# Attention-done pairs take turns with the others in the last loop, with their digits on two halves of the partitions

## The chip, the core and the metric

The kernel runs on one core of a Trainium2 chip. The metric is the device time of one execution in microseconds (us), given as the median of several runs. A profiled execution has a span, which is some 1.8 us shorter than the time of the same run; spans and starts below are from profiles, medians from timed runs.

TensorE multiplies matrices (PE in the profile), VectorE (DVE) and ScalarE (ACT) work on elements, GpSimd (POOL) issues the loads of this kernel, SyncE (SP) the stores. PSUM is the memory that TensorE writes to.

## The reference

```python
# q, k, v: (8 batches, 8 heads, 576, 64); s: (8, 8, 576)
scores = q @ k^T / 8 + min(-(cum_i - cum_j), 0), causal      # cum = cumsum(max(s, 0))
x = softmax(scores) @ v                                      # as (8, 576, 512)
X = rfft(x, axis=1)[:, :64]                                  # 64 modes
Y = X @ (w_r + i w_i), one 512x512 matrix for each mode      # 128 MB of weights
u = x + irfft(Y)
out = u + max(u @ w_ch, 0)                                   # (8, 576, 512)
```

The kernel uses that u @ w_ch = x @ w_ch + irfft(Y @ w_ch). The product x @ w_ch can therefore be made before the last weight of the modes is there, and be kept until Y is complete.

## The kernel before

The output is cut into 18 pairs of row tiles (128 rows each; two of the 18 are tail pairs, made of 64-row ends). Pairs 0 and 1 are done by themselves. The other 16 have their product x @ w_ch kept in SBUF and added back in a last loop. A kept product has one of two forms: fp32, which ScalarE copies back into PSUM ("s"), or two fp16 digits, high and rest, which TensorE adds back with an identity matrix ("e").

```python
ways = dict(zip(kept, "esesessesesseses"))            # kept = pairs 2 to 17

def keep_product(i, xx, z):                            # z is the product in PSUM
    if ways[i] != "e":
        nc.scalar.copy(out=z1s[i][:, xx], in_=z)
        return
    nc.scalar.copy(out=z1s[i][:, 0, xx], in_=z)        # high digit
    nc.vector.tensor_tensor(out=z1s[i][:, 1, xx], in0=z, in1=z1s[i][:, 0, xx], op=ALU.subtract)
```

Attention runs in 32 steps (0 to 31). In the last six, the channel product of a pair that attention has finished is squeezed in, one half before and one half behind the product with the mode weights:

```python
for n in range(N):                                     # N = 32 steps
    load(loads_qkv(n + LA) + tails_due, loads_w(on_chip[n]))   # GpSimd issues
    ...
    av(n, 0)
    if i is not None:
        first_product(i, 0)                            # 4 matmuls, keep_product
        first_transposed(i, 1)
    for c in mode_steps.get(n, []):
        modes(c // NCK, c % NCK)                       # 16 matmuls on 4 weight tiles
    if i is not None:
        first_product(i, 1)
```

All these write into one pool of two PSUM buffers, so the mode product needs the buffer that keep_product is still reading. The weights come in tiles of 512 KB through a ring (WA = 11 tiles at this stage); a tile can be issued only when the mode product has used the one that lay in its place.

The last loop, in which each pair gets its z (the product, relu'd later) and u (x and the inverse transform):

```python
def seed(i):
    ...
    if ways.get(i) == "s":
        nc.scalar.copy(out=zs[i], in_=z1s[i])
    elif ways.get(i) == "e":
        for x in range(2):
            for y in range(2):
                nc.tensor.matmul(zs[i][:, x, :], ident16h, z1s[i][:, y, x, :],
                                 start=(y == 0), stop=False, ...)

for i in range(NPRE, len(pairs)):
    pre(i)                          # seed if "e", then two matmuls of the inverse transform
    start_u(i)
    add_y(us[i], i, 0)
    if ways.get(i + 1) == "s":
        seed(i + 1)                 # on ScalarE, ahead of this pair's relu
    if ways[i] != "v":
        relu(i, 2 if i == last else 1)      # ScalarE
    finish(i)                       # VectorE adds u and the relu, then the store
```

The softmax here doesn't subtract the row's maximum and nothing guards it: scores larger than these inputs give would overflow.

## Time and profile before

| before | value | from |
|---|---|---|
| time, median | 459.26 us (458.73 to 459.38) | 3 runs |
| span of the profiled run | 457.1 us | page |
| last weight lands | 418.07 | load's issue and landing |
| last loop on TensorE | 424.07 to 451.88 | chain of waits |
| mean clock granted to TensorE, 300 to 350 us | 1.00 | stretches |

The table of stretches of the kernel before, over the last steps of attention (stretch in us; then length, busy us and instructions of TensorE, weight loads, VectorE, ScalarE, GpSimd; granted clock; share of the DMA engines; GB/s):

```profile
300.00:320.00 20.00, 17.95 (x258) 12.30 (x258) 13.05 (x27) 11.65 (x22) 10.56 (x15) 1.00 1.31 202
320.00:340.00 20.00, 16.27 (x213) 11.09 (x215) 12.43 (x30) 11.21 (x22) 6.79 (x10) 1.00 1.24 206
340.00:360.00 20.00, 15.76 (x137) 8.56 (x141) 10.94 (x18) 4.04 (x6) 5.94 (x8) 0.91 1.24 212
```

TensorE is busy for 80 to 90% of the time, and the transfers go at 202 to 212 GB/s. TensorE's timeline of the kernel before, the mode products of steps 29 and 30 (start, length, what; in brackets the idle time before it and what ended that):

```profile
316.21 1.12 PE L441 MATMUL yp<-w_sb,xs 128*32 128x512 bf16 x16 [0.45 <-ACT z L491]
...
326.13 1.13 PE L441 MATMUL yp<-w_sb,xs 128*32 128x512 bf16 x16 [0.45 <-ACT z L491]
```

An "s" product lets the mode product go after 0.45 us; behind an "e" product, in steps 28 and 31, the wait was 1.18. GpSimd's timeline of the kernel before, the loads that waited for steps 30 and 31:

```profile
326.92 0.75 POOL L217 DMA_DIRECT2D w_sb<-in_moe_w_i_dram  x1 [5.33 <-PE yp L441]
...
336.58 0.74 POOL L217 DMA_DIRECT2D w_sb<-in_moe_w_i_dram  x1 [5.58 <-PE yp L441]
```

GpSimd waits 5 us for the ring. The tile issued at 326.92 lands at 342.44, 15.5 us later, since five other tiles have still to land ahead of it.

### The profile page before, as it was taken

Reading aid. Unit: us, or ns where it says so; the run is one execution under the profiler, and the core shown is the slowest. Engines: PE = TensorE matmul, PEld = TensorE weight load, DVE = VectorE, ACT = ScalarE, POOL = GpSimd, SP = SyncE. Lnnn points to the kernel's source line nnn. Section 1 sums busy time; section 2 is a strip of 40 time slices with the busy share of each in tenths; the row PEclk is TensorE's granted clock in tenths of the full one; section 3 lists DMA queues with packets and bytes.
Section 4 is the critical chain, followed back from the end, with each engine's and each line's share of the span. In section 5 each row is a group of like instructions: output and inputs, shape, how many; then the busy total and the mean of one; then the engine's idle time right before and its main releaser. Section 6 shows DMA issues by size and latency. Waiting matters only on the chain.

```text
span 457.1 us, 10262 instructions
## 1 busy us (share of the span) xinstructions
PE 339.1 (74%) x4177; PEld 217.2 (48%) x4209; DVE 237.3 (52%) x528; ACT 219.1 (48%) x382; POOL 182.9 (40%) x269
## 2 busy tenths in 40 slices
PE   1779968966562979936587766779967769797995
PEld 1556646644341656614355544446643326343432
DVE  7777645653242556624345544466656425442675
ACT  1587856554241747723445345446622220221895
POOL 6755555544345555344454444355423223200000
PEclk9999999998586889957778799899999778999999
DMA  9999999999999999999999999999999999995688
GB/s 177 201 203 203 202 201 204 202 204 204 204 204 201 202 202 202 204 205 204 199 192 205 204 204 204 204 203 202 207 206 212 210 210 210 214 214 105 235 285 319
DMA packets 109375, 94.54 MB, mean 207 GB/s; under 512 B 28480, under 2 KB 104512, under 8 KB 109328
## 3 DMA queue, kind: packets, MB, share of 16 engines
q0 software_dynamic: 98960, 81.81, 113.0%
q1 hardware_dynamic: 10368, 12.07, 8.5%
q8 instruction: 33, 0.54, 0.4%
q14 instruction: 14, 0.11, 0.1%
HBM read 164.56 MB, written 9.44 MB: 381 GB/s over the span
## 4 chain that ended last, share of the span: by engine, by line
DMA 70%; PE 20%; issue 4%; POOL 3%; DVE 2%; DVEq 0%; POOLq 0%
DMA w_sb<-in_moe_w_i_dram 44%; DMA q<-in_q_dram 13%; DMA w_sb<-in_moe_w_r_dram 5%; PE yp L441 3%; PE sc_ps L365 3%; PE av_ps L394 2%; DMA x_all<-in_moe_w_r_dram 2%; DMA k<-in_k_dram 2%; PE sc_ps L359 2%; DMA y_acc<-in_moe_w_i_dram 2%; PE tr_ps L324 2%; DMA y_acc<-in_moe_w_r_dram 2%; PE u_ps L694 2%; PE z_ps L675 2%; PE u_ps L675 2%
## 5 line engine op out<-in xcount | busy, mean ns | idle before, releaser
L373 ACT ACTIVATE p_sb<-sc_ps,cumt_sb 128x576 f16<-128x576 f32 (+1 forms) x256 | 141.9, 636 | 45.8 <-PE sc_ps L365 45.4
L217 POOL DMA_DIRECT2D w_sb<-in_moe_w_i_dram x60 | 45.1, 751 | 81.7 <-PE yp L441 36.8
L217 POOL DMA_DIRECT2D w_sb<-in_moe_w_r_dram x60 | 45.4, 757 | 65.2 <-DMA w_sb<-in_moe_w_r_dram 26.1
L217 POOL DMA_DIRECT2D v<-in_v_dram x72 | 50.8, 707 | 31.3 <-DMA w_sb<-in_moe_w_r_dram 8.4
L324 PE MATMUL tr_ps<-ident,q 64*64 64x64 bf16 x576 | 17.1, 208 | 55.4 <-DMA q<-in_q_dram 55.4
L359 PE MATMUL sc_ps<-negm,ident 128*128 128x256 bf16 x256 | 55.0, 300 | 0.3
L441 PE MATMUL yp<-w_sb,xs 128*32 128x512 bf16 x480 | 37.0, 408 | 22.2 <-DMA w_sb<-in_moe_w_i_dram 18.1
L327 DVE COPY qtA<-tr_ps 64x576 bf16<-64x576 bf16 x32 | 23.8, 743 | 50.8 <-PE tr_ps L324 50.7
L344 ACT ACTIVATE p<-sc_ps,cumt 128x64 f16<-128x64 f32 x32 | 10.1, 314 | 74.2 <-PE sc_ps L340 74.2
L394 PE MATMUL av_ps<-v,p_sb 128*128 128x65 f16 x1024 | 43.7, 196 | 0.0
L394 PEld LDWEIGHTS <-p_sb 128*128 128x128 f16 x1024 | 38.9, 99 | 4.8 <-issue 0.7
L327 DVE COPY ktA<-tr_ps 64x576 bf16<-64x576 bf16 x32 | 24.0, 750 | 32.7 <-PE tr_ps L324 32.7
L324 PEld LDWEIGHTS <-q 64*64 64x64 bf16 x576 | 13.3, 120 | 58.0 <-DMA q<-in_q_dram 56.9
L441 PEld LDWEIGHTS <-xs 128*32 128x32 bf16 x512 | 22.9, 169 | 32.3 <-issue 28.8
L365 PE MATMUL sc_ps<-qtB,ktB 128*128 128x64 bf16 (+2 forms) x160 | 34.8, 322 | 3.7 <-issue 2.4
L365 PE MATMUL sc_ps<-qtA,ktA 65*128 65x512 bf16 (+2 forms) x192 | 36.1, 297 | 0.3 <-DVE ktA L327 0.3
L399 DVE TENSOR_REDUCE den<-av_ps 128x5 f32<-128x10 f32 x64 | 10.8, 169 | 46.4 <-PE av_ps L394 46.4
L404 DVE TENSOR_TENSOR x_all<-av_ps,rcp 128x320 f16<-128x320 f32 x64 | 31.5, 492 | 2.2
L327 ACT COPY ktB<-tr_ps 64x576 bf16<-64x576 bf16 x32 | 20.3, 634 | 19.7 <-DVE ktA L327 18.8
L365 PEld LDWEIGHTS <-ktB 128*128 128x128 bf16 x192 | 22.4, 117 | 14.8 <-issue 6.3
L324 PE MATMUL tr_ps<-ident,k 64*64 64x64 bf16 x576 | 17.5, 210 | 14.0 <-DVE qtB L327 10.5
L601 PE MATMUL z_ps<-wch_sb,xs 128*128 128x512 f16 x96 | 26.2, 423 | 0.8 <-DVE xs L595 0.8
(112 smaller groups left out, 526.4 us busy)
## 6 DMA issues: line engine op xcount, KB each, us to landing
w_sb<-in_moe_w_r_dram POOLq DMA_DIRECT2D x60, 512.0 KB, 11.9
w_sb<-in_moe_w_i_dram POOLq DMA_DIRECT2D x60, 512.0 KB, 11.9
q<-in_q_dram POOLq DMA_DIRECT2D x32, 144.0 KB, 9.7
k<-in_k_dram POOLq DMA_DIRECT2D x32, 144.0 KB, 10.1
v<-in_v_dram POOLq DMA_DIRECT2D x72, 64.0 KB, 9.7
out_dram<-r_sb SPq DMA_DIRECT2D x16, 256.0 KB, 2.3
out_dram<-r_w SPq DMA_DIRECT2D x16, 256.0 KB, 2.6
x_all<-in_moe_w_i_dram POOLq DMA_DIRECT2D x3, 512.0 KB, 10.0
```

Source lines behind the costliest of these rows:

```text
L217: nc.gpsimd.dma_start(out=dst, in_=src)
L324: nc.tensor.transpose(ps[rows, r, :], src[rows, r, :], ident16[rows, rows])
L327: copy(out=dst[n % NQ][rows, :].rearrange("d (p r) -> d p r", r=R), in_=ps[rows].rearrange("d r p -> d p r"),)
L359: nc.tensor.matmul(ps[:, bass.ds(w * S, W)], ident16, negm[:, bass.ts(r, W)], start=True, stop=False, skip_group_check=True,)
L365: nc.tensor.matmul(ps[:, c0 : c0 + i1 - i0], keys[:, w, r, :], qt[:, i0:i1], start=False, stop=True, skip_group_check=True,)
L373: nc.scalar.activation(out=pt[:, poff[x] : poff[x] + S - w * W], in_=ps[:, w * S : (w + 1) * S - w * W], func=ACTF.Exp, bias=cumt_sb[:, x, ...
L394: nc.tensor.matmul(ps[:, I, r : r + NCH], lhsT, rhs, start=(i == 0), stop=(i == len(todo) - 1), skip_group_check=True,)
L399: nc.vector.tensor_reduce(out=den, in_=ps[:, :, 0 : VW : NCH], axis=mybir.AxisListType.X, op=ALU.add)
L404: nc.vector.tensor_tensor(out=x_all[:, g, b, :, D * h : D * h + D], in0=ps[:, :, 1 : NCH], in1=rcp.unsqueeze(2).to_broadcast([P, NT, D]), ...
L441: nc.tensor.matmul(ps[32 * cg : 32 * cg + 32, :], cols[:, c0 : c0 + 32, c * MC + 2 * cg + par], wt[(g, c, ri, par)][:, cg, :], start=(x == ...
L601: nc.tensor.matmul(z[:, x, :], xts[i][:, x, dt, :], wch_sb[:, dt, :], start=(dt == 0), stop=(last and dt == DT - 1), skip_group_check=True,)
L675: nc.tensor.matmul(dst[x][r, :], G_sb[rows, bass.ds(T * P, r.stop - r.start)], yv[rows, bb, which, :], start=start, stop=True, skip_group_ ...
```

## The change

Its intent is a shorter last loop. An "e" seed costs TensorE four full matmuls. The change introduces a third form, "f": the high digit of rows 0 to 63 lies on the lower half of the partitions and the rest digit of the same rows on the upper half; for rows 64 to 127 it is the other way round. A folding matrix of 128 x 64 adds high and rest in one matmul, and two such matmuls run side by side on two groups of 64 columns. The six pairs whose product is made in attention become "f", one late pair (place 15) is "e", all others are "s"; and the order of the loop is changed so that "f" and "s" pairs alternate.

```diff
+    ident16h_np = np.concatenate([ident_np, ident_np[:, : P // 2] + ident_np[:, P // 2 :]], axis=1)
...
-    pairs = [((b, T), (b, T + 1)) for b in range(B) for T in range(0, NF, 2)]
-    for i, b in ((4, 0), (10, B // 2)):
-        pairs.insert(i, ((b, NF), (b + 2, NF)))
+    turns = [whole[1] + whole[2] + whole[3], whole[4] + whole[5] + whole[6] + whole[7]]
+    turns[1].insert(1, tail_pairs[0])
+    turns[1].insert(5, tail_pairs[1])
+    pairs = list(whole[0])
+    for t in turns[1]:
+        pairs.append(t)
+        if turns[0]:
+            pairs.append(turns[0].pop(0))
...
-    ways = dict(zip(kept, "esesessesesseses"))
+    first_pairs = [i for i in kept if pairs[i][0][0] in (1, 2, 3) and pairs[i][0][1] < NF]
+    ways = {i: "f" if i in first_pairs else "s" for i in kept}
+    for i in (15,):
+        ways[i] = "e"
...
     def keep_product(i, xx, z):
...
+            for y in range(2):
+                own, other = (slice((P // 2) * h, (P // 2) * (h + 1)) for h in (y, 1 - y))
+                nc.scalar.copy(out=z1s[i][own, y, xx], in_=z[own])
+                nc.vector.tensor_tensor(
+                    out=z1s[i][other, y, xx], in0=z[own], in1=z1s[i][own, y, xx], op=ALU.subtract
+                )
...
+        elif ways.get(i) == "f":
+            for x in range(2):
+                for y in range(2):
+                    nc.tensor.matmul(
+                        zs[i][(P // 2) * y : (P // 2) * (y + 1), x, :], fold16h, z1s[i][:, y, x, :],
+                        start=True, stop=False, skip_group_check=True,
+                        tile_position=(0, (P // 2) * y),
+                    )
```

More of the change, by code (lines that the diff above doesn't have):

```diff
@@ L77 @@
     G_np = G_np.reshape(P, SP).astype(np.float16)
-    d_ident16h = nc.inline_tensor(ident_np.astype(np.float16), name="c_ident16h").ap()
+    ident16h_np = np.concatenate([ident_np, ident_np[:, : P // 2] + ident_np[:, P // 2 :]], axis=1)
+    d_ident16h = nc.inline_tensor(ident16h_np.astype(np.float16), name="c_ident16h").ap()
     d_ident32 = nc.inline_tensor(ident_np, name="c_ident32").ap()
@@ L98 @@
     xs = [gp.tile([P, 5, 2, B, NM], BF16, name=f"xs{i}") for i in range(2)]
-    ident16h = gp.tile([P, P], FP16, name="ident16h")
+    ident16h2 = gp.tile([P, P + P // 2], FP16, name="ident16h")
+    ident16h, fold16h = ident16h2[:, :P], ident16h2[:, P:]
     Ff_sb = gp.tile([P, NT, 3 * NM], FP16, name="Ff_sb")
@@ L249 @@
     nc.sync.dma_start(out=Ff_sb, in_=d_Ff.rearrange("(T p) c -> p T c", p=P))
-    nc.sync.dma_start(out=ident16h, in_=d_ident16h)
+    nc.sync.dma_start(out=ident16h2, in_=d_ident16h)
     nc.sync.dma_start(out=G_sb, in_=d_G)
@@ L465, in spread @@
         nc.sync.dma_start(out=yv[16 * c : 16 * c + 16, :, which, :], in_=rows)
-    pairs = [((b, T), (b, T + 1)) for b in range(B) for T in range(0, NF, 2)]
-    for i, b in ((4, 0), (10, B // 2)):
-        pairs.insert(i, ((b, NF), (b + 2, NF)))
+    whole = [[((b, T), (b, T + 1)) for T in range(0, NF, 2)] for b in range(B)]
+    tail_pairs = [((b, NF), (b + 2, NF)) for b in (0, B // 2)]
+    turns = [whole[1] + whole[2] + whole[3], whole[4] + whole[5] + whole[6] + whole[7]]
+    turns[1].insert(1, tail_pairs[0])
@@ L473 @@
+    turns[1].insert(5, tail_pairs[1])
[4 more added lines that the diff above has]
+            pairs.append(turns[0].pop(0))
     NPRE = 2
     kept = list(range(NPRE, len(pairs)))
-    ways = dict(zip(kept, "esesessesesseses"))
-    first_pairs = [i for i in kept[1:] if pairs[i][0][1] < NF and pairs[i][0][0] <= 4][:6]
+    first_pairs = [i for i in kept if pairs[i][0][0] in (1, 2, 3) and pairs[i][0][1] < NF]
+    ways = {i: "f" if i in first_pairs else "s" for i in kept}
@@ L480, with keep_product @@
+    for i in (15,):
+        ways[i] = "e"
     z1s, xts1 = {}, {}
     def kept_place(i, t):
-        if ways[i] == "e":
+        if ways[i] == "s":
+            z1s[i] = t.bitcast(FP32).rearrange("p (x e) -> p x e", x=2)
+        else:
             z1s[i] = t.bitcast(FP16).rearrange("p (y x e) -> p y x e", y=2, x=2)
-        else:
-            z1s[i] = t.bitcast(FP32).rearrange("p (x e) -> p x e", x=2)
-    def keep_product(i, xx, z):
-        if ways[i] != "e":
-            nc.scalar.copy(out=z1s[i][:, xx], in_=z)
-            return
-        nc.scalar.copy(out=z1s[i][:, 0, xx], in_=z)
-        nc.vector.tensor_tensor(out=z1s[i][:, 1, xx], in0=z, in1=z1s[i][:, 0, xx], op=ALU.subtract)
+    def keep_product(i, xx, z):
+        if ways[i] == "s":
+            nc.scalar.copy(out=z1s[i][:, xx], in_=z)
+        elif ways[i] == "e":
+            nc.scalar.copy(out=z1s[i][:, 0, xx], in_=z)
+            nc.vector.tensor_tensor(
+                out=z1s[i][:, 1, xx], in0=z, in1=z1s[i][:, 0, xx], op=ALU.subtract
+            )
+        else:
+            for y in range(2):
+                own, other = (slice((P // 2) * h, (P // 2) * (h + 1)) for h in (y, 1 - y))
+                nc.scalar.copy(out=z1s[i][own, y, xx], in_=z[own])
+                nc.vector.tensor_tensor(
+                    out=z1s[i][other, y, xx], in0=z[own], in1=z1s[i][own, y, xx], op=ALU.subtract
+                )
@@ L800, in seed @@
     def seed(i):
-        if ways.get(i) in ("e", "s"):
+        if ways.get(i) in ("e", "f", "s"):
             zs[i] = zpool.tile([P, 2, DM], FP32, name="z_ps", tag="z")
@@ L811, in seed @@
                     )
+        elif ways.get(i) == "f":
[5 more added lines that the diff above has]
+                        tile_position=(0, (P // 2) * y),
+                    )
     def pre(i):
-        if ways[i] == "e":
+        if ways[i] in ("e", "f"):
             seed(i)
```

## The prediction

> **What bounds the kernel now.** I read the slices of the page first, then the chain that ended last, then the two stretches of that chain which the change touches: the last loop and the last six steps of attention.
>
> ```profile
> DMA  9999999999999999999999999999999999995688
> GB/s 177 201 203 203 202 201 204 202 204 204 204 204 201 202 202 202 204 205 204 199 192 205 204 204 204 204 203 202 207 206 212 210 210 210 214 214 105 235 285 319
> ```
>
> The transfers are busy and move a near constant 200 to 214 GB/s for 36 of 40 slices. The chain, cut to the end, says where that stops:
>
> ```profile
> 396.06 22.01 DMA w_sb<-in_moe_w_i_dram
> 418.07 0.04 issue
> 418.11 0.48 PE yp L441 x4
> ...
> 424.07 0.86 PE z_ps L808 x4
> 424.93 0.43 PE z_ps L675 x2
> 425.36 0.43 PE u_ps L694 x2
> 425.80 0.43 PE u_ps L675 x2
> ...
> 438.51 0.55 PE z_ps L675 x4
> 439.06 0.55 PE u_ps L694 x4
> 439.61 0.55 PE u_ps L675 x4
> 440.16 0.97 PE z_ps L808 x4
> ```
>
> Columns: start, length, what. The last weight lands at 418.07. About 6 us of fixed tail follow, then the last loop (16 kept pairs) from 424.07 to 451.88. The stretches table shows TensorE solid there:
>
> ```profile
> core 0: us, PE busy (x) PEld busy (x) DVE busy (x) ACT busy (x) POOL busy (x), PEclk, DMA share, GB/s
> ...
> 424.07:451.90 27.83, 27.82 (x136) 11.42 (x134) 19.93 (x32) 24.50 (x26) 0.00 (x0) 1.00 0.84 298
> ```
>
> So two regimes: weight arrival until 418, TensorE from 424 to 452, at full clock; 5.2 us of last addition, writing out and ending follow. Work before 418 costs nothing unless it lets the weight queue run empty.
>
> **What the Trainium skill says.** TensorEngine Tiling (Array Packing), Key Properties: tiles work independently, and "Changing tiling mode (not just tile) drains the TensorE". The trace agrees in size: a tail pair's four matmuls on two 64-column groups take 0.55 us, against 2 x 0.2155 = 0.431 for two full ones. Two of the four run at a time, plus about 0.115 us a change of mode, paid again on the way out (0.97 instead of 0.86 at 440.16). Perfetto Trace Analysis, Optimization Strategy: kernels can have regimes with different most-contended engines; that is the split above. VectorE: DVE Perf Modes, Why PSUM operands drop a tier: an fp32 operand in PSUM runs at 1x. The 128x512 subtract at 0.69 us agrees, and as free size sets it, I expect half the partitions to save nothing.
>
> **The last loop.** A whole pair is 6 matmuls, 3 x 0.431 = 1.295 us. A tail pair is 3 x 0.55 + 0.11 = 1.76. An "e" seed adds 4 matmuls, 0.863. Before: 14 x 1.295 + 2 x 1.76 + 7 x 0.863 = 27.7, measured 27.8. So the sum works, and stalls are nil.
>
> After, by the built order: six "f", one "e", nine "s". An "f" seed is 2 x 0.2155 + 0.115 in + 0.115 out = 0.66, and two of the six follow a tail pair already in 64-column mode, which saves 0.23 each. Sum: 18.13 + 3.52 + 6 x 0.66 - 0.46 + 0.86 = 26.0, which is 1.7 less. ScalarE's load is unchanged (nine seeds and sixteen relus, 24.5 us busy), and it fits: an s-f turn is 3 of its instructions, at starts 0.92 to 1.05 apart, about 2.95, against 2 x 1.295 + 0.66 = 3.25 on TensorE. VectorE has 4 adds, 2.6.
>
> But the loop now opens with an "s" pair instead of an "e". Its seed can start on ScalarE only behind the relu of pair 1, which started at 422.91; so about 423.85, and ready at 424.9. TensorE, in order, idles from 424.07: a new stall of 0.85 us. Net gain of the loop: 1.7 - 0.85 = **0.85 us**. At the end pair 17 is an "s" as before, with the same relu, add and write, so the gain should reach the end.
>
> **The last six attention steps.** There the kept product was one 128x512 copy on ScalarE for four of the six pairs, copy plus subtract for two. Now each half pair takes two copies and two subtracts, and the built program makes the second copy wait for VectorE, so I take the four as serial: 0.59 + 0.69 + 0.59 + 0.69 plus about 0.05 a hop = 2.7 us, against 0.6 ("s") or 1.3 ("e"). Here is what that meets:
>
> ```profile
> 335.79 1.12 PE L441 MATMUL yp<-w_sb,xs 128*32 128x512 bf16 x16 [1.18 <-DVE z L494]
> ```
>
> ```profile
> 328.27 0.59 ACT L491 COPY z<-z_ps 128x512 f32<-128x512 f32 x1 [2.19 <-PE z_ps L513]
> 328.93 2.21 ACT L373 ACTIVATE p_sb<-sc_ps,cumt_sb 128x576 f16<-128x576 f32 x4
> ```
>
> The first fence is TensorE's timeline, the second ScalarE's (start, length, what, in brackets the idle time before it and its releaser). The mode product waited 1.18 us for the digits to leave its PSUM buffer (two buffers, shared); after an "s" copy it was 0.45. The exponentials of the next step start directly behind the copy of the second half. So per step, first half: 2.07 us (from "s") or 1.33 (from "e") more wait for the mode products. Second half: ScalarE is held 1.3 us longer, copy plus the wait for a subtract plus copy less the one copy, and the next step's second scores wait on those exponentials. That is 3.4 us a step from "s", 2.6 from "e".
>
> What absorbs it? Steps 26 and 27 waited for q and k anyway:
>
> ```profile
> 287.50 0.47 PE L324 MATMUL tr_ps<-ident,q 64*64 64x64 bf16 x18 [2.92 <-DMA q<-in_q_dram]
> ...
> 299.88 0.47 PE L324 MATMUL tr_ps<-ident,q 64*64 64x64 bf16 x18 [2.04 <-DMA q<-in_q_dram]
> ```
>
> Steps 28 to 31 have no such wait. Counting forward: all of step 26 is absorbed, about 1.3 us of 27 is left, 28 adds 2.6, 29 and 30 add 3.4 each, and 31 adds 1.3 to its mode product: some **12 us** late, attention ending near 352 instead of 340.
>
> Is that hidden? The weight ring holds 11 tiles, and a slot comes free with the mode product. The tile issued at 336.58, directly after the last mode product of step 31, lands at 353.18, and the one ahead of it in the queue at about 350.7. Issued 12 us later, at 348.5, it is still about 2 us ahead of an empty queue. The step before is as close: issue 326.92 goes to about 336.1, the queue ahead lasts to about 339.0. So the transfers should just not run dry, but an error of 3 us in my count would cost 1 to 2 us. After attention TensorE is busy 59.6 of 76.1 us up to the last weight; of the 16.5 idle us most are waits for weights, so a 12 us delay can be caught up, barely. I charge 0.8 us in the mean for these two edges.
>
> Elsewhere nothing: late "e" products fall from five to one, which frees VectorE of 4 x 1.23 us while it waits for weights; the identity constant is half as large again, 48 KB for 32, at the start.
>
> **Sum.** 459.26 - 0.85 + 0.8 = 459.2 us.
>
> **Rivals.** (1) The intent alone: the loop shortens and attention's delay is hidden; 458.4, or 457.6 if the opening stall is also mended by order. For it: the transfers' 10 to 20 us from issue to landing, and compute that waits on weights after 342. Against: the delay counted above uses nearly all of that lead. (2) The weight queue runs dry in steps 29 to 31, since a step of 13.3 us releases four tiles that transfer in 10.4 (four of about 2.6 us): 461 to 463. For it: the count; against: the second copy's wait may be on something older than the subtract, and then two copies and two subtracts overlap and half of the delay vanishes. (3) The column groups don't overlap, or ScalarE becomes the loop's bound: an "f" seed of 0.86 + 0.23 in series makes the sum 28.6 and the loop, with its opening stall, 1.8 us longer: 461. Against: the tail pairs have just this shape (128 rows, 64 columns, two groups in turn) and take 0.55; ScalarE has 0.3 us of slack a turn. For: that slack is small, and relu, seed, add_y form a chain through two PSUM buffers. (4) The writing out bounds the loop, which already runs at 298 GB/s of output, peaks near 400; worth at most some tenths at the end.
>
> **Range and chances.** A gain of 0.85 (0.3 to 1.3) against a loss of 0 to 4, skewed to one side, and runs of before 0.65 us apart: 457.8 to 462.2. Two per cent is 9.2 us; no mechanism above reaches it, save a queue dry for several steps. Faster 0.01, within 0.97, slower 0.02.
>
> **What would show it.** In the trace of after: "f" seed of x4 at 0.55 to 0.66 us; TensorE idle about 0.85 us before the first z_ps of the loop; loop end to end 26.9 us; ScalarE's 64-row copies and VectorE's 64-row subtracts at 0.59 and 0.69 each and alternating in time; mode products waiting about 2.5 us for the subtract; last av_ps of attention near 350 instead of 338.5; GB/s between 300 and 355 without a hole. It is wrong if the last weight lands more than 1 us away from 418, if an "f" pair costs TensorE 2.1 us or more, or if ScalarE, not TensorE, has no gaps in the loop.

## More of the kernel before

ScalarE's and VectorE's timelines of the kernel before at the very end:

```profile
448.91 1.02 ACT L804 COPY z_ps<-z 128x1024 f32<-128x1024 f32 x1
449.96 1.02 ACT L713 ACTIVATE r_sb<-z_ps 128x1024 f32<-128x1024 f32 x1
```

```profile
451.02 2.48 DVE L728 TENSOR_TENSOR r_sb<-u_ps,r_sb 128x512 f32<-128x512 f32 x4 [0.82 <-ACT r_sb L713]
```

The copy at 448.91 is the seed of pair 17, the activation at 449.96 the relu of pair 16, and the last four adds of VectorE start behind it. From there to the end of the span it is 6.0 us.

## The result, and the profile after

The changed kernel is correct and takes 464.14 us (median of 6 runs, 463.16 to 465.15), against 459.15 (458.64 to 459.38) for the kernel before on the same chip. The ratio is 1.011, interval 1.009 to 1.013: 5 us slower. A ratio here is the mean time of one kernel's fast runs over that of the other's of the same rounds, so not quite the ratio of the medians that are quoted.

One caution on the traces: the profiled run of after has a span of 463.4 and is the slowest of its six (the spans go from 461.4 to 463.4), the profiled run of before with 457.1 is an ordinary one. So some 1 us of the 6.3 between the two traces is the luck of that run.

**Where the time went.** The last weight lands at 424.70 instead of 418.07, 6.6 us later. From the start of the last mode product to the end of the span it is 38.7 us instead of 39.0. So the loop gave 0.3 us, and everything else was lost before the last weight. The slices of the page of after:

```profile
GB/s 176 201 203 203 201 203 203 203 204 204 204 205 198 204 201 204 204 204 205 200 196 204 204 204 205 202 203 202 192 166 142 209 210 213 210 217 124 223 334 272
```

Slices 29 to 31 hold 192, 166 and 142 where before had 207, 206 and 212 (a slice is 11.6 us). That is a shortfall of 15, 40 and 70 GB/s over 11.6 us each, 1.45 MB; at 209 GB/s some 7 us of transfer. The hole is about as large as the whole loss. By the landings of the loads the lag on before is 1.5 us at the load that was issued at 338.61 (it lands at 343.91 for 342.44) and 4.6 at the one issued at 352.44 (357.71 for 353.14); the last 2 us of the 6.6 come in small steps after that, which I have not taken apart. The stretches of after, the first three of them the same as those shown of before, the last one the loop:

```profile
300.00:320.00 20.00, 16.33 (x208) 10.51 (x208) 12.93 (x27) 12.07 (x23) 9.17 (x14) 0.83 1.30 202
320.00:340.00 20.00, 13.88 (x176) 8.41 (x175) 13.37 (x29) 10.03 (x19) 4.37 (x6) 0.94 1.12 182
340.00:360.00 20.00, 12.74 (x119) 7.18 (x118) 9.62 (x22) 8.08 (x15) 4.56 (x7) 0.84 1.00 161
...
430.70:457.72 27.02, 26.18 (x137) 9.96 (x136) 19.50 (x31) 24.20 (x26) 0.00 (x0) 1.00 0.87 300
```

The transfers fall to 182 and then 161 GB/s, as TensorE gets through fewer instructions (176 matmuls for 213 from 320 to 340), and the clock is 0.83 and 0.94 up to 340, where it was 1.00 (then 0.84 for 0.91). Behind the mode products stand the waits, in TensorE's timeline of after:

```profile
310.52 1.96 PE L444 MATMUL yp<-w_sb,xs 128*32 128x512 bf16 x16 [2.50 <-DVE z L516]
...
324.81 1.12 PE L444 MATMUL yp<-w_sb,xs 128*32 128x512 bf16 x16 [2.50 <-DVE z L516]
...
337.62 1.97 PE L444 MATMUL yp<-w_sb,xs 128*32 128x512 bf16 x16 [2.50 <-DVE z L516]
...
351.45 1.96 PE L444 MATMUL yp<-w_sb,xs 128*32 128x512 bf16 x16 [2.50 <-DVE z L516]
...
431.55 0.59 PE L699 MATMUL z_ps<-yv,G_sb 128*128 128x512 f16 x2 [0.84 <-ACT z_ps L828]
```

Each of these steps waits 2.50 us for the second subtract. And three of the four mode products then take 1.96 us in place of 1.12; the granted clock was 0.50 from 310.52 to 312.48 and 1.00 in the step at 324.81. The waits are the serial chain of two copies and two subtracts, as ScalarE's timeline (its second copy) and VectorE's (both subtracts) of after show for step 30:

```profile
336.26 0.58 ACT L515 CAST z<-z_ps 64x512 f16<-64x512 f32 x1 [0.75 <-DVE z L516]
```

```profile
335.54 0.68 DVE L516 TENSOR_TENSOR z<-z_ps,z 64x512 f16<-64x512 f32 x1 [0.66 <-ACT z L515]
336.87 0.69 DVE L516 TENSOR_TENSOR z<-z_ps,z 64x512 f16<-64x512 f32 x1 [0.65 <-ACT z L515]
```

The first copy runs from 334.93 to 335.51, the subtract from 335.54 to 336.22, the second copy from 336.26, the second subtract from 336.87: one after the other. The second copy waits 0.75 us for the first subtract, although it uses nothing that the subtract makes. Half the partitions save no time: 0.58 and 0.69 us, as for 128. What the delay does to the ring is in GpSimd's timeline of after:

```profile
338.61 0.74 POOL L220 DMA_DIRECT2D w_sb<-in_moe_w_i_dram  x1 [10.04 <-PE yp L444]
...
352.44 0.74 POOL L220 DMA_DIRECT2D w_sb<-in_moe_w_i_dram  x1 [10.46 <-PE yp L444]
```

These are the two loads shown of before, 11.7 and 15.9 us later. The second is issued when nothing is left in the queue: the load ahead of it landed at 351.76. It lands after 5.3 us in flight, where in before the same load took 16.6.

The loop itself did what it should on TensorE: 26.18 us busy for 27.82, with one stall of 0.84 us at its head (the line at 431.55). The chain of after shows the new seeds:

```profile
433.01 0.55 PE z_ps L839 x4
433.56 0.54 PE z_ps L699 x2
...
436.62 0.43 PE z_ps L839 x4
```

Four matmuls in 0.55, with 0.11 us more on the way out (0.54 for the two that follow instead of 0.43), and 0.43 behind a tail pair. But the end of after, in ScalarE's and VectorE's timelines:

```profile
455.36 1.02 ACT L828 COPY z_ps<-z 128x1024 f32<-128x1024 f32 x1
456.31 1.99 ACT L737 ACTIVATE r_sb<-z_ps 128x1024 f32<-128x1024 f32 x3
```

```profile
457.36 2.48 DVE L752 TENSOR_TENSOR r_sb<-u_ps,r_sb 128x512 f32<-128x512 f32 x4 [0.71 <-ACT r_sb L737]
```

Pair 16 is now an "s", so TensorE has its z ready sooner. Its matmuls start at 454.97 and are done 0.6 us later, at 455.57, but its relu starts at 456.31: ScalarE is busy until then with the seed of pair 17, which stands ahead in its queue. TensorE ends its loop 33.02 us after the last weight instead of 33.81 (0.79 gained), the last adds start 32.66 us after it instead of 32.95 (0.29 gained).

### The profile page after: what moved, and what is told of

Read it like the earlier page. It is cut to its first block, busy times and chain, and to the rows that moved or that the text cites. A ratio compares the mean times of both kernels' runs of the same rounds, so it can differ in the third digit from the quotient of the medians.

```text
span 463.4 us, 10303 instructions
## 1 busy us (share of the span) xinstructions
PE 346.2 (75%) x4177; PEld 217.5 (47%) x4209; DVE 246.0 (53%) x544; ACT 225.6 (49%) x394; POOL 182.7 (39%) x269
## 4 chain that ended last, share of the span: by engine, by line
DMA 50%; PE 30%; DVE 9%; ACT 4%; issue 3%; POOL 2%; SPq 0%; DVEq 0%; POOLq 0%; ACTq 0%
DMA w_sb<-in_moe_w_i_dram 26%; DMA q<-in_q_dram 10%; DMA k<-in_k_dram 9%; PE yp L444 4%; PE av_ps L397 4%; PE sc_ps L368 3%; PE tr_ps L327 3%; PE z_ps L537 3%; PE sc_ps L362 2%; ACT z L515 2%; PE ft_ps L421 2%; DVE z L516 2%; DMA w_sb<-in_moe_w_r_dram 2%; PE z_ps L625 2%; PE z_ps L699 2%
## 5 line engine op out<-in xcount | busy, mean ns | idle before, releaser
L362 PE MATMUL sc_ps<-negm,ident 128*128 128x256 bf16 x256 | 57.1, 310 | 3.8 <-ACT p_sb L376 3.3
L444 PE MATMUL yp<-w_sb,xs 128*32 128x512 bf16 x480 | 39.0, 442 | 21.1 <-DVE z L516 12.5
L397 PE MATMUL av_ps<-v,p_sb 128*128 128x65 f16 x1024 | 44.7, 198 | 0.0
L368 PE MATMUL sc_ps<-qtA,ktA 65*128 65x512 bf16 (+2 forms) x192 | 39.0, 315 | 0.3 <-DVE ktA L330 0.3
L444 PEld LDWEIGHTS <-xs 128*32 128x32 bf16 x512 | 21.4, 173 | 32.0 <-issue 15.6
L368 PE MATMUL sc_ps<-qtB,ktB 128*128 128x64 bf16 (+2 forms) x160 | 33.7, 315 | 3.3 <-issue 2.0
L402 DVE TENSOR_REDUCE den<-av_ps 128x5 f32<-128x10 f32 x64 | 10.8, 169 | 40.3 <-PE av_ps L397 39.9
L515 ACT CAST z<-z_ps 64x512 f16<-64x512 f32 x24 | 13.9, 579 | 37.0 <-PE z_ps L537 28.0
## 6 DMA issues: line engine op xcount, KB each, us to landing
w_sb<-in_moe_w_r_dram POOLq DMA_DIRECT2D x60, 512.0 KB, 11.7
```

Source lines behind the costliest of these rows:

```text
L362: nc.tensor.matmul(ps[:, bass.ds(w * S, W)], ident16, negm[:, bass.ts(r, W)], start=True, stop=False, skip_group_check=True,)
L368: nc.tensor.matmul(ps[:, c0 : c0 + i1 - i0], keys[:, w, r, :], qt[:, i0:i1], start=False, stop=True, skip_group_check=True,)
L397: nc.tensor.matmul(ps[:, I, r : r + NCH], lhsT, rhs, start=(i == 0), stop=(i == len(todo) - 1), skip_group_check=True,)
L402: nc.vector.tensor_reduce(out=den, in_=ps[:, :, 0 : VW : NCH], axis=mybir.AxisListType.X, op=ALU.add)
L444: nc.tensor.matmul(ps[32 * cg : 32 * cg + 32, :], cols[:, c0 : c0 + 32, c * MC + 2 * cg + par], wt[(g, c, ri, par)][:, cg, :], start=(x == ...
L515: nc.scalar.copy(out=z1s[i][own, y, xx], in_=z[own])
```

## The experiments

The theory: the cost of making the halved digits in attention delays the mode products, the ring frees its tiles late, the weight queue runs dry, and the half clock after each stall makes the delay larger than its waits. The rivals: the new order of the loop is to blame; or the "f" seeds themselves; or the loss is only the waits, and the clock is a bystander.

All twelve kernels gave correct results, and by the 2% rule all are the same as before, save after_ring10, which is unclear. "Before" is the kernel before. The last column but one is the start of the last mode product in the profiled run, the last one the time from there to the end of the span (before: 418.11 and 39.0; after: 424.74 and 38.7).

| kernel | median (range) us | before | ratio (95%) | last mode product | to the end |
|---|---|---|---|---|---|
| e_for_f | 460.42 (460.23 to 460.72) | 460.11 | 1.001 (0.9997 to 1.003) | 418.37 | 40.3 |
| before_f | 467.0 (464.43 to 467.32) | 460.11 | 1.014 (1.011 to 1.017) | 421.89 | 40.8 |
| copies_first | 462.6 (462.14 to 463.94) | 460.11 | 1.0065 (1.004 to 1.009) | 422.64 | 38.7 |
| deferred | 462.86 (462.19 to 463.48) | 460.11 | 1.007 (1.005 to 1.009) | 421.63 | 38.8 |
| after_warm | 460.35 (459.64 to 460.78) | 459.34 | 1.002 (0.999 to 1.005) | 419.86 | 38.6 |
| after_ring10 | 466.97 (466.13 to 469.28) | 459.34 | 1.017 (1.014 to 1.021) | 426.41 | 38.7 |
| before_ring10 | 459.7 (458.72 to 460.25) | 459.34 | 1.000 (0.998 to 1.003) | 418.17 | 38.8 |
| deferred2 | 464.08 (463.55 to 464.41) | 459.34 | 1.010 (1.008 to 1.012) | 423.51 | 38.8 |
| deferred3 | 461.28 (460.3 to 462.25) | 459.65 | 1.003 (1.0005 to 1.006) | 421.52 | 38.8 |
| def3_f_first | 459.34 (458.7 to 460.88) | 459.65 | 1.000 (0.997 to 1.003) | 418.40 | 38.5 |
| def3_f_first2 | 459.7 (459.17 to 460.81) | 459.65 | 1.000 (0.998 to 1.002) | 419.37 | 38.0 |
| before_late_f | 459.68 (458.5 to 459.96) | 459.41 | 0.999 (0.997 to 1.001) | 419.75 | 37.9 |

### The order alone: e_for_f

The kernel after, with the plain digits in place of the halved ones.

```diff
-    ways = {i: "f" if i in first_pairs else "s" for i in kept}
+    ways = {i: "e" if i in first_pairs else "s" for i in kept}
```

> The changed kernel, with plain e digits (one copy, one subtract, full width) for the six pairs done in attention; the order of the pairs stays. Theory (attention): hold of the buffer 1.3 us instead of 2.7, nothing extra on ScalarE; attention 3 to 5 us later than before, inside the ring's lead, so the last weight at 418 to 419; the loop has 7 e seeds as before (27.7 us) plus the opening stall of 0.85 and the slower end of about 0.5: 459.6 to 461. Rival (order): if the order of the pairs is the cause, above 463.

The last mode product is at 418.37, as before, and the ratio is 1.001. The mode product of step 31 comes at 337.15, 1.4 us later than in before (3 to 5 had been expected). So neither the new order nor digits as such (one copy, one subtract, and a wait of 1.2 us for the mode product) run the queue dry. The last part is 1.6 us longer than in after, which is what six "e" seeds cost more than six "f" seeds.

### The halved digits alone: before_f

The kernel before with its own order and its own late pairs; the six attention pairs are made "f".

```diff
+    for i in first_pairs:
+        ways[i] = "f"
```

> The kernel before, its order of pairs kept, only the six pairs done in attention made f (two halves, column groups). Theory (attention): the delay is that of the changed kernel, last weight at 423 to 425.5; the loop has 6 f and 5 e seeds, 1.5 to 2 us more TensorE than before: 465 to 468. Rival (order): the last weight at 418 and 460 to 461.5.

The loss is there without the new order: ratio 1.014. The profile fell on the fastest of its four runs (464.43) and has its last mode product at 421.89, earlier than expected; the other three are some 2.6 us slower. The mode products wait 2.50 us here too. This run and the one above pin the loss on making the halved digits in attention.

### Half of the chain: copies_first

Both copies are put ahead of both subtracts, so that the second copy need not wait for a subtract.

```diff
+            half = [slice((P // 2) * h, (P // 2) * (h + 1)) for h in range(2)]
+            for y in range(2):
+                nc.scalar.copy(out=z1s[i][half[y], y, xx], in_=z[half[y]])
             for y in range(2):
-                own, other = (slice((P // 2) * h, (P // 2) * (h + 1)) for h in (y, 1 - y))
-                nc.scalar.copy(out=z1s[i][own, y, xx], in_=z[own])
                 nc.vector.tensor_tensor(
-                    out=z1s[i][other, y, xx], in0=z[own], in1=z1s[i][own, y, xx], op=ALU.subtract
+                    out=z1s[i][half[1 - y], y, xx], in0=z[half[y]], in1=z1s[i][half[y], y, xx],
+                    op=ALU.subtract,
                 )
```

> The changed kernel with both ScalarE copies issued ahead of both VectorE subtracts, so that the second copy doesn't wait for a subtract. Theory (attention): ScalarE is held 1.1 instead of 1.9 us, the buffer about 2.3 instead of 2.7: about 1 us less a step, attention some 5 us less late, and about half of the 6.6 us comes back: 460.5 to 462.5, last weight at 420 to 422.5. Rival (the amount of VectorE and ScalarE work, not its serial order, is what counts): no change, 463.5 to 464.5.

The last weight lands 2.1 us earlier than in after (422.60), and the ratio falls from 1.011 to 1.0065. But it is not the wait in front of the mode product that got shorter, as TensorE's timeline of this kernel shows:

```profile
337.64 1.13 PE L444 MATMUL yp<-w_sb,xs 128*32 128x512 bf16 x16 [2.46 <-DVE z L517]
```

It is 2.46 us for 2.50: the first subtract starts only when both copies are done (336.20; the copies run from 334.99 to 336.16). What went are TensorE's waits for the exponentials, 0.95 to 1.35 us in three steps of after and none here, since ScalarE is free sooner behind the second half. So the time for which ScalarE is held is part of the delay; the wait in front of the mode product this run left as it was, and the gain came out a little under what was expected. This is also a better form of the change as written.

### The clock: after_warm

In each of the last six steps ten matmuls whose result nobody reads are put into a free PSUM buffer, where TensorE waits anyway. Nothing of the copies and subtracts is changed.

```diff
+                junk = trpool.tile([P, DM], FP32, name="junk", tag="tr")
+                for x in range(10):
+                    nc.tensor.matmul(junk, ident16h, Ff_sb.rearrange("p T c -> p (T c)")[:, :DM],
+                                     start=True, stop=True, skip_group_check=True)
             for c in mode_steps.get(n, []):
```

> The changed kernel with ten needless full-width matmuls (2.2 us at full clock) into an otherwise idle PSUM buffer, placed just ahead of the mode products of the last six attention steps, where TensorE stood idle for 2.5 us. They fill the stall and delay nothing of use. Theory (clock): in the changed kernel most such stalls were followed by matmuls at half clock (mode products 1.96 instead of 1.12 us, products with the channel weights 1.7 instead of 1.04), which is why the delay came to 15.7 us and not to the 12 I counted. With the stalls filled the clock stays at 1.0 from 300 to 350, attention comes 9 to 12 us late, the last weight at 419.5 to 422.5, the total 2 to 4 us under the changed kernel's: 460 to 462.5. Rival (clock dips come from load, not from idling): as many dips or more, 464 or above.

The stretch from 300 to 350 us of this kernel, then its mode product of step 31 in TensorE's timeline:

```profile
300.00:350.00 50.00, 43.45 (x514) 26.79 (x514) 33.90 (x69) 29.02 (x54) 17.69 (x25) 1.00 1.24 199
```

```profile
346.62 1.12 PE L444 MATMUL yp<-w_sb,xs 128*32 128x512 bf16 x16 [0.34 <-DVE z L516]
```

The clock stays at 1.00 (after: 0.90 in the same stretch), the mode product takes 1.12 us again, and the channel product behind it 1.04, where after's second channel products took 1.7 to 1.9 in five of the six steps. The mode product of step 31 comes at 346.62, 10.8 us later than in before; in after it comes 15.7 later. So the waits alone cost 10.8 us in attention, and the half clock behind them another 4.8. The last weight lands at 419.82 instead of 424.70. The profiles differ by 4.9 us, the medians by 3.8; the 1.1 between them is the slow profile of after. This run decides the question of the clock: with the waits untouched, keeping TensorE busy through them takes back three quarters of the loss.

The Trainium skill, TensorE: Matmul & The Clock Gate, Part 1: The HAM clock gate, says that TensorE's clock falls to half when it idles, in windows of some 3.4 us that run freely, and gives (under HAM oscillation) as the rule to keep gaps under some 3.4 us. The trace agrees with the factor (granted clock 0.50; the mode product takes 1.96 for 1.12, which is 1.75). It does not agree with the threshold: gaps of 2.50 us were followed by slow matmuls in three of the four steps shown. Nor does the length of the gap decide alone: in before_f, with the same gaps, two of the five mode products were slow. What decides is worked out under why the prediction was wrong.

### The ring: after_ring10 and before_ring10

```diff
-    WA, WB = 11, 6
+    WA, WB = 10, 6
```

> The changed kernel with a weight ring of 10 tiles instead of 11. Theory (the ring starves): each tile now waits for a mode product one tile later, so the gap in the transfers grows by about one tile's time, 2.6 us: last weight at 426.5 to 428, total 466 to 468. Rival (the delay reaches the end through TensorE's own backlog, not through the ring): unchanged within 0.7, 463.5 to 465.

> Control for the ring of 10: the kernel before with it. Theory: its attention is early by some 11 us against the ring's lead, so losing 2.6 of them costs nothing: within 0.5 us of before, last weight at 418. Rival (a shorter ring slows the transfers anyway): 1 us or more slower, and the run of the changed kernel with a ring of 10 would say nothing.

One tile less costs the changed kernel 2.8 us (466.97 for 464.14; in the profiles the last weight lands at 426.36 for 424.70) and the kernel before nothing (1.000). So the changed kernel has used up the lead that the ring gives, and the kernel before has at least one tile of it to spare.

### Digits made after attention: deferred, deferred2, deferred3

If the delay in attention is all that is wrong, the digits can be made elsewhere. In attention only one fp32 copy leaves PSUM; while TensorE later waits for weights, the digits are made from that copy in SBUF.

```diff
-            for y in range(2): ...                      # two copies, two subtracts
+            nc.scalar.copy(out=z32[i][:, xx], in_=z)
...
+    def split(i):
+        for x in range(2):
+            d, src = free.pop(), z32[i][:, x]
+            ...                                          # two copies, then two subtracts
+    SPLIT = (0, 1, 1, 1, 2, 1)                           # pairs split beside each late mode product
...
+        for x in range(SPLIT[c]):
+            split(to_split.pop(0))
```

> The changed kernel, but in attention each kept product leaves PSUM by one ScalarE copy in fp32, as an s pair does; the digits are made from that copy after attention, beside the weight waits. Theory (attention): the four serial digit instructions held the PSUM buffer 2.5 us a step, attention came 15.7 us late and the weight ring starved. Then here the last weight lands within 0.7 us of before (418.1 against 424.7), attention ends near 342, and the total is that of before less what the loop gives: 458.6 to 459.3. Rival (loop): the new order and the column groups cost the 5 us themselves, and the total stays above 462.

The landing was as expected, the time was not. The last weight lands at 417.95 and the transfers have no hole, but the last mode product comes at 421.63, and the ratio is 1.007 where I had hoped for a gain. TensorE's timeline of this kernel shows a new stall, VectorE's timeline what stood before it:

```profile
401.95 0.61 PE L660 MATMUL yt_ps<-ident16h,y_sb 128*128 128x128 f16 x4 [5.38 <-DVE y_sb L458]
```

```profile
392.32 1.40 DVE L595 TENSOR_TENSOR z<-z,z 64x512 f16<-64x512 f32 x2 [2.55 <-ACT z L593]
393.83 1.40 DVE L595 TENSOR_TENSOR z<-z 64x512 f16<-64x512 f32 x2
...
401.22 0.68 DVE L458 TENSOR_TENSOR y_sb<-yp,y_acc 128x512 f16<-128x512 f32 x1
```

VectorE first waits 2.55 us for the copies of the splits and then does two pairs of splits, from 392.32; the y_sb for which TensorE waits stands behind all this and starts at 401.22. The same page of the Trainium skill, in the section Architectural detail of Part 1, calls the queues of ScalarE and VectorE strict FIFO; this is what it looks like. So this experiment takes away one cause and puts in another, and only the landing of the weights is evidence for the theory.

deferred2 splits half pairs in another spread (SPLIT 2, 3, 3, 0, 2, 0, and two inside the first product with w_ch):

> As the run with digits made after attention, but the digits come in half pairs, placed where VectorE is idle (behind the work of modes 0 to 2 and 4, and two within the product of the first modes), since there two of them in a row held the addition of the sixth mode product back by 5.4 us. Theory: the last weight at 418 as there, and now the last mode product with it; the total is before less the 0.25 to 0.85 us of the loop: ratio 0.998 to 1.000, 458.5 to 459.5 at a before of 459.2. Rival (the f loop is itself slower): 460.5 or more.

It missed: no hole in the transfers, but the waits for y_sb from 342 to 420 come to 9.7 us (before: 2.4), and the ratio is 1.010. deferred3 splits whole pairs as early as possible (2, 1, 2, 1, 0, 0):

> Digits after attention once more, as whole pairs: two behind mode product 0, one behind 1, two behind 2, one behind 3, none near the end, since in the first such run the pairs behind mode products 1 to 3 cost no wait that showed and those behind the fifth cost 5.4 us. Theory: last weight at 418 and the last mode product with it, so that only the loop is left: 0.1 to 0.9 us under before, ratio 0.998 to 1.000. Rival (VectorE's queue holds TensorE back wherever the digits stand): 1.003 or more.

It missed, as its rival had it: 1.003, with 8.6 us of waits for y_sb and a last mode product at 421.52, 3.4 us after the last weight landed at 418.11.

### Mending the head of the loop: def3_f_first, def3_f_first2

These are deferred3 with the turns reversed, so that the loop begins with an "f" pair that needs no ScalarE, and with an "e" at place 16 (in the second also at 14), so that the relu of pair 16 does not queue.

```diff
+        if turns[0]:
+            pairs.append(turns[0].pop(0))
         pairs.append(t)
-        if turns[0]:
-            pairs.append(turns[0].pop(0))
...
-    for i in (15,):
+    for i in (16,):                                      # (14, 16) in the second
```

> The same with the turns the other way round (the loop begins with an f pair, whose seed needs no ScalarE) and the one e pair moved from place 15 to 16, so that the end is e, s as before. Theory: the opening stall of 0.85 us goes, and relu 16 no longer queues behind a seed; the loop gives 1.2 to 1.8 us against before: ratio 0.996 to 0.998, if the digits cost nothing. Rival: ScalarE takes over (s, s, s at 13 to 15), no better than the run with the order kept.

> The same with two e pairs, at 14 and 16. Theory: one seed less on ScalarE, 0.86 us more on TensorE; no pair of s in a row after 13. Within 0.6 us of the run with one e; better than it only if ScalarE bound the end there.

TensorE's timeline of the first of the two, at the head of the loop:

```profile
424.31 0.41 PE L854 MATMUL z_ps<-xs,ident16h 128*64 128x512 f16 x2
```

No idle time stands before the first seed of the loop: the opening stall is gone. TensorE's loop ends 1.2 us sooner after the last weight than in before (450.94 - 418.32 = 32.62 for 33.81), yet the span is only 0.1 us shorter and both kernels equal the kernel before (1.000), so the gain expected of the first is missed. The traces show where the rest goes: VectorE's last adds start 1.2 us sooner after the last weight too (450.08), but the last store, issued at 452.79, takes 2.9 us to land, where before's, issued at 453.53, took 2.3. From 452 to 454 the transfers go at 382 GB/s here and at 319 in before. So the writing out, rival (4) of the prediction, takes most of what this loop gains; no run moved it by itself. In the second one the last part is 0.9 us shorter and the last mode product 1.3 us later.

### Halved digits where there is time: before_late_f

The last try keeps attention and the order as before and halves only the five digits that are made late (places 2, 4, 11, 14, 16), with the copies ahead of the subtracts.

```diff
+    for i in kept:
+        if ways[i] == "e" and i not in first_pairs:
+            ways[i] = "f"
```

> The kernel before, with its order and all attention pairs as they were; only the five products that are kept after attention, late, as two digits (places 2, 4, 11, 14, 16) lie on two halves of the partitions and are added by two column groups. Both copies stand ahead of both subtracts. Theory (the halved digits were made at the wrong time; the digit making costs nothing where TensorE waits for weights anyway, the seed is a gain wherever it lies): attention's mode products at the times of before, last weight within 0.5 us of 418.1. Loop: five seeds of 0.86 become three of 0.66 and, beside the tail pairs at places 4 and 10, two of 0.43, in all 0.6 + 0.86 = 1.5 us less TensorE; some 0.5 to 1.0 of that reaches the end, since relu 16 now stands closer behind the last copied seed. Ratio 0.997 to 0.999. Rival (found in the deferred runs: each late digit split holds VectorE or ScalarE in front of something that the late mode products wait for): two half copies and two half subtracts of 128x1024 take 2.0 and 2.4 us in place of 1.0 and 1.2, five times, and the last mode product comes 1 to 3 us late although the weights are there: ratio 1.001 to 1.005.

The seed is the gain it was counted to be: TensorE's loop goes from 425.74 to 452.08, 26.3 us for 27.8, and the last part is 1.1 us shorter. But the last mode product comes at 419.75, 1.6 us late (the last weight itself lands at 419.12, 1.0 late), and the ratio is 0.999 with an interval that includes 1. In TensorE's timeline of this kernel:

```profile
406.85 3.17 PE L618 MATMUL z_ps<-wch_sb,xs 128*128 128x512 f16 x8 [2.91 <-DVE xs L612]
```

In before this product waited 0.56 us for VectorE and took 1.90. Here it waits 2.91 for VectorE, which has one more subtract a pair to do, and then takes 3.17: the longer wait and the slower matmuls after it, again in one line. Both theory and rival were half right.

## Why the prediction was wrong

The prediction was 459.2 us in a range of 457.8 to 462.2. The result, 464.14, lies outside. It said "within 2%" with 0.97, which held. By its steps:

- **The wait of the mode products** (predicted "about 2.5 us for the subtract"): right, 2.50 in every step shown, with copies and subtracts of 0.58 and 0.69 in series.
- **"some 12 us late"**: too small. Step 31's mode product came 15.7 us late. The mechanism was right: with the clock held up, the same waits gave 10.8, so the count itself was 1.2 too high. What was missing is a term that the prediction did not have at all. It took TensorE's instructions at the durations of before, at full clock, while the stalls that it had itself counted put the clock to half for what came after them: a mode product 1.96 for 1.12, a channel product 1.7 to 1.9 for 1.04. after_warm puts this term at 4.8 us.
- **"So the transfers should just not run dry"** and **"I charge 0.8 us"**: this is the step that failed. They ran dry by some 7 us of transfer; the last weight came 6.6 us late. The prediction had itself said that issued at 348.5 the tile "is still about 2 us ahead of an empty queue", and that 3 us of error would cost 1 to 2. The issue came at 352.44 instead of 348.5. The error was 3.9 us, and it also hit the step before (338.61), so there were two holes and not one.
- **The margin** was wrong as well as the delay. The prediction took a tile to be in time if it is issued before the one ahead has landed. The tile issued at 338.61 was 1.55 us ahead of that (340.16), and still landed 3.75 us behind it, where tiles of a full queue follow each other by 2.5 to 2.6. A tile that meets an empty queue is 5.3 us in flight, so by these figures (my estimate) it has to be issued some 2.7 us before the one ahead lands. (The prediction's 339.0 for the end of the queue ahead in the step before is misread too: in before that load lands at 339.90.) The size of the lead comes out of four runs, with step 31's mode product and the last weight each against before: 10.8 us of delay cost 1.8 us in after_warm, 13.2 cost 3.8 in before_f, 14.2 cost 4.5 in copies_first, 15.7 cost 6.6 in after. Delay less cost is 9.0 to 9.6 in all four: the lead was some 9.3 us where the prediction counted 14 (350.7 - 336.58), and behind it each us of delay costs about one. By that, even the predicted 12 us would have cost 2.7 us and not 0.8.
- **"so a 12 us delay can be caught up, barely"**: it could not, but not for the reason given. TensorE did catch up: from slice 32 on the transfers ran at 209 to 217 GB/s again, and the last mode product followed its weight at once. But the transfers were at that rate in before too, so the time they had lost could not be won back.
- **The loop**: "1.7 less" was 1.64 (27.82 to 26.18), the "f" seed 0.55 + 0.11 and 0.43 behind a tail pair as counted, the opening stall 0.84 for 0.85. At TensorE's end 0.79 of the predicted 0.85 us was there.
- **"the gain should reach the end"**: it did not; 0.29 us did. The prediction looked at pair 17, which is unchanged. Pair 16 went from "e" to "s", its relu came to stand behind the seed of pair 17 on ScalarE, and the last adds wait for that relu. The 0.3 us of slack that it had counted for a turn of ScalarE was not there in the last one.
- **The rivals**: (2), the dry queue, was the right one, with 461 to 463 still too low, for the same missing clock and the lead counted too long. (1) falls with the hole in the transfers, (3) by the seeds of 0.55; (4) plays no part in after, whose last store lands after 2.3 us as in before, but shows in def3_f_first.

Why the clock dipped in three of four steps and not in the one at 324.81 can be read from the clock of after. Between 305 and 355 us its half-clock stretches begin at 310.33, 337.64 and 351.29, 8 and 4 times 3.41 us apart, and last 3.41 us. In the other traces the stretches are whole multiples of 3.41 us too, but lie at other times (288.46 to 291.87 in before): windows that run freely, as the skill has it. Three pairs of such windows (columns as in the stretches above):

```profile
306.92:310.33 3.41, 1.10 (x8) 0.50 (x6) 2.04 (x5) 1.52 (x3) 1.89 (x4) 1.00 1.31 203
310.33:313.74 3.41, 3.22 (x20) 1.12 (x21) 1.52 (x3) 0.00 (x0) 1.46 (x2) 0.50 1.31 201
...
320.57:323.98 3.41, 1.74 (x23) 1.00 (x19) 2.05 (x7) 1.86 (x4) 0.00 (x0) 1.00 1.26 203
323.98:327.40 3.42, 2.59 (x26) 1.51 (x27) 2.07 (x3) 0.52 (x2) 1.80 (x3) 1.00 1.10 178
...
347.88:351.29 3.41, 1.07 (x8) 0.50 (x6) 2.04 (x5) 1.16 (x2) 0.00 (x0) 1.00 1.13 188
351.29:354.70 3.41, 3.25 (x20) 1.17 (x21) 1.49 (x3) 0.00 (x0) 2.26 (x4) 0.50 0.18 20
```

Where nearly all of a stall lies in one window (TensorE busy for 1.10 and 1.07 of 3.41 us), the next window is at half clock. The stall before 324.81 lies across two windows and leaves 1.74 us busy in the first: no dip. In all fourteen traces, from 275 to 356 us, each of the 29 windows at full clock in which TensorE was idle for 1.88 us or more was followed by half clock, 6 of the 16 with 1.4 to 1.88, and 1 of the 207 with less. So which of the stalls were followed by a dip is luck of where they fell; no run moved one on purpose.

## What to carry to other kernels

An idle gap in front of TensorE has to be counted twice where the clock is granted by activity: once for the wait, once for the matmuls after it (1.75 times their time here); a fill of useless matmuls in the gap tells the two apart, and may be worth keeping. Work on buffers that a ring of transfers waits for costs nothing until the lead of the ring is used up and then everything, so compare the issue times with the end of the queue ahead, with an allowance (a tile that met an empty queue took 5.3 us to land here), and test the lead by taking one buffer away. Moving work to where an engine looks idle is not free either: in queues that run in order, what counts is which instruction stands behind it.

## What the Trainium skill lacked or had wrong

- TensorE: Matmul & The Clock Gate, Part 1: The HAM clock gate: the window of 3.41 us agrees, but the rule of gaps over some 3.4 us is too generous. Gaps of 2.50 us put the clock down in three of four steps (1.96 us for 1.12), and a gap of 2.91 us did in before_late_f (3.17 us for 1.90); filling the 2.50 us with matmuls kept 1.00. The page speaks of short idle times in another kernel, but gives no length; here 1.88 us or more within one window were followed by half clock in 29 of 29 cases.
- TensorEngine Tiling (Array Packing), Key Properties: says that changing the tiling mode drains TensorE, without a cost. Here a change cost 0.11 us on the way in and again on the way out (four matmuls 0.55, the next two 0.54, against 0.43 without a change).
